# Kernel matmul steps kept a least distance apart in the planned order, with the planner's durations replaced and the third tile's arguments 128 columns wide

## The chip, the cores and the metric

The kernel runs on one core of a Trainium2 chip. The metric is the device time of one execution in microseconds. The kernel before was run three times: 387.19, 384.06 and 383.83 us, median 384.06 us. The profile is of a fourth, separate execution.

## The reference

The input is 2048 rows of width 640. Two branches work on it and a sigmoid gate of the input mixes them. The first branch is attention with 32 heads of width 20, in which row `s` looks at the eight rows `s, s-2, ..., s-14`. The second is a state-space convolution: per channel a kernel `K` of length 2048 is made from 192 complex modes, and the input is convolved with it by FFT.

```python
q, k, v = split(x @ wqkv)                        # 32 heads of 20
kg, vg = k[idx], v[idx]                          # idx = s - 2*w, w = 0..7
attn = softmax(where(mask, q . kg * 20**-0.5, -1e9))
a = (sum_w attn * vg) @ wo
P = exp(dt * A * l)                              # 640 channels x 192 modes x 2048
K = einsum("dn,dnl,dn->dl", C, P, dt * B).real
y = irfft(rfft(x, 4096) * rfft(K, 4096))[:2048] + x * Dskip
out = g * a + (1 - g) * y                        # g = sigmoid((x * gate_w).sum(-1))
```

## The kernel before

One launch holds two parts. The first part, some 300 us long, is planned: every piece of work is a `Task` with the engine it may run on, a duration, what it depends on, the buffers it takes and gives back, and a due time. `Plan.order` plays all tasks against a model of the engines, and `Plan.emit` writes the instructions in the order in which they were played and chains each engine's instructions to that order. So the instruction streams of TensorE, VectorE, ScalarE, GpSimd and the SP queue are fixed when the program is built. The durations and the numbers in `PLAN` (due times, and the small shifts `off`) decide the order and are not executed. In that model TensorE work is lengthened where too little of it (`eq`, counted in windows of 3.4133 us) was played in the window before.

The second part, some 80 us, is the FFT convolution and the final mix (`fft_conv`). It is written out by hand, is the same in both kernels and starts when the planned part has ended.

The planned part holds these streams, which share the engines:

- **Parameters** (`SSMParams.build`): elementwise work on VectorE and ScalarE over the mode parameters. It ends in twelve pieces `S`, written to memory through the SP queue.
- **Projections** (`turn`, `late`): the input is turned on TensorE, then 60 steps of five 128x512 matmuls give q, k and v (line 328). They are evicted by ScalarE or VectorE (lines 490 and 492), stored and read back by GpSimd's DMA queue.
- **Attention core**, eight blocks of 256 rows (`plan_core`): five `prod` products on VectorE (line 377) and their `lg` matmuls (383), the softmax (`max` on VectorE, `neg` on TensorE, `exp` on ScalarE at line 407, `sum` on TensorE, `at` on VectorE), a round trip through memory on the SP queue (`aS`, `asb`), five `pv` products (442), the gathering matmuls `gat` (447), the output projection `wo` (464) and its gated eviction `ga`.
- **Kernel generation**, ten chunks (`KGen.plan`). A chunk's parameters `L` are loaded by eight DMAs on the SP queue. Then, for three tiles `u` = 0, 1, 2, the argument matmuls `arg` (lines 768 and 773, into the two `ar` buffers) feed ScalarE, which takes sines (line 785) and exponentials (787). When a tile has both, VectorE makes products `pq` (808 to 810, two buffers), and four steps `kmm` per tile (826) multiply them on TensorE into the one buffer `kps`. After the third tile `fin` copies `kps` into `E` (1179) and frees it for the next chunk. Sine and exponential need different tables on ScalarE, so each change between them is a table load; the softmax needs the exponential too.
- **Expansion and first FFT stage**: after chunks 4 and 9 the sums are expanded (`own`, `move` with `nxp` at line 864, `other`), written to memory, read back as `kc`, and multiplied by a constant (`f1`, `fu`, `fk`, result `bp`, line 1195).

A tile is 128 rows of parameters wide. The parameter buffer holds 192 modes twice, so tiles 0 and 1 have 128 modes of one half each, and tile 2 is made of the remaining 64 modes of both. In the kernel before tile 2's arguments take two matmuls of 64 columns where the others take one of 128:

```python
if u < 2:      # one matmul of 128 columns
    nc.tensor.matmul(ar[:, g2, ...], L[rows, gp, sb, NST * u:NST * u + 128], R[...], tile_position=(64 * g2, 0))
else:          # two of 64
    for h in range(2):
        nc.tensor.matmul(ar[64 * h:64 * h + 64, g2, ...], L[rows, h, sb, m0:m0 + 64], R[...], tile_position=(64 * g2, 64 * h))
```

A `kmm` step of tiles 0 and 1 is 16 matmuls of 128 rows, one of tile 2 is 32 matmuls of 64 rows, each with its own weight load. The planner may play these steps as soon as the products are there, so several can stand one behind the other on TensorE.

Of the kernel before, what the change touches and what calls it, by code (L numbers as in the profile page):

```python
# [20 lines left out]
S = 2048  # L21
D = 640
H = 32
DH = 20
W = 8
# [11 lines left out]
def _attn_consts():  # L37
# [5 lines left out]
    for wp in range(W):  # L43
# [4 lines left out]
PLAN = dict(free=dict(P=4.0, A=4.2, D=4.7, S=16.0, G=16.0), phase=0.0, look=0.2, ba=85.1, bd=-687.6, grace=2235.8, p0=-791.4, p1=9.6, tx=[1364.4, 1460.7],  # L48
            txw=191.1, ql=135.4, vl=-242.7, pw=18.0, el=-653.5, tl=53.4, vw=216.1, gate=2445.0,
            l=[281.2, 189.1, 532.1, 186.3, 592.1, 47.7, -314.8, 735.8, 829.8, 993.2, 720.0, 710.4], a=[363.0, -174.6, -128.2, 185.6, 703.1, 918.9, 1303.1, 1413.4],  # L50
            v=[-164.3, -448.6, 45.4, 323.3, 710.0, 789.4, 646.8, 1095.8], g=[10.7, 292.0, -348.6, -469.5, -539.5, 427.8, 247.2, -1193.3, -158.0, -278.7, -66.5],
            dl=[129.5, 80.5, 337.8, 725.2, 614.9, 306.3, 515.6, 330.1, 400.6, 420.8],
            kl=[-352.8, -363.0, -133.2, -213.8, -584.9, -123.6, 147.3, -7.2, -17.6, -95.2], Ll=1248.1, argl=366.8, xl=1038.4, c0=1194.1, x0=1143.6, x1=118.9,
            f0=-483.5, f1=51.4, u0=914.8, u1=33.6, off={59: 46.6, 61: 84.7, 94: -58.1, 96: -12.9, 100: -8.6, 102: -29.5, 107: 10.3, 111: 11.8, 113: 8.0, 116: -14.8,
# [14 lines left out]
class Plan:  # L69
# [25 lines left out]
    def order(self):  # L95

        pr = self.pr
# [15 lines left out]
        act, table, W, done = {}, None, 3.4133, []  # L113

        def ready(t):
            x = t.rdy
            for tag in t.acq:
                k = cnt[tag] - self.SLOTS[tag]
                if k >= 0:
                    if k not in gone[tag]:  # L120
                        return None
                    x = max(x, gone[tag][k])
            return x
        for t in self.tasks:
            t.rdy = t.rdy0
        while len(done) < len(self.tasks):
# [38 lines left out]
            t.start, t.eng = x, e  # L165
            free[e] = x + d
# [38 lines left out]
class Attn:  # L205
# [22 lines left out]
    def window(self, pl, cst, pa):  # L228
# [7 lines left out]
        for n in range(2 * NKT):  # L236
            hf, kt = divmod(n, NKT)
            b = {}

            def turn(_, hf=hf, kt=kt, b=b):  # L240
                tx = b["tx"] = pa.tile([128, 2, 512], F32, name="ar")
                for i in range(8):
                    nc.tensor.matmul(tx[:, i // 4, (i % 4) * 128:(i % 4) * 128 + 128], self.xn[:, 8 * hf + i, kt * 128:(kt + 1) * 128], self.ident[:], start=True, stop=True)  # L243

            def ev(en, hf=hf, kt=kt, b=b):
                evict(nc, en, self.xT[:, hf, kt, :], b["tx"][:].rearrange("p a b -> p (a b)"))
            d = pl.pr["tx"][hf] + pl.pr["txw"] * kt
            m = pl.add(f"turn{n}", "P", 0.75, turn, acq=["ar"], due=d, eq=1024, rdy=(16.5, 26.0)[hf])
            self.xts.append((m, pl.add(f"tev{n}", "AD", {"A": 1.0, "D": 1.2}, ev, deps=[m], rel=[("ar", m)], due=d + 0.5)))
# [97 lines left out]
    def plan_core(self, pl, pvb, g_sb, ps, due0):  # L347
# [10 lines left out]
        for sc in range(S // C):  # L358
# [68 lines left out]
            sm = pl.add(f"sum{sc}", "P", 0.40, total, deps=[ex], due=due(5 * pr["pw"] + pr["el"]), eq=512)  # L427
# [4 lines left out]
            for e in range(0, 5, 2):  # L432
# [20 lines left out]
                p = lastpv = pl.add(f"pv{sc}{e}", "D", 1.11 * n, weigh, deps=[asb, vc], after=[lastpv], acq=["pv"], rel=[("vc", vc), ("asb", asb)] if e == 4 else [], due=due(pr["v"][sc] + pr["vw"] * e))  # L453
# [41 lines left out]
NST = 192  # L495
# [213 lines left out]
class KGen:  # L709
# [24 lines left out]
    def load_L(self, c):  # L734
        nc = self.nc
        L = self.Lb[c % 2]
        for g in range(4):
            for v in range(2):
                d0 = 160 * g + 80 * v + 8 * c
                src = self.prm.S[d0:d0 + 8].rearrange("(s q) i n -> (q i) s n", q=4)  # L740
                nc.sync.dma_start(L[64 * (g % 2) + 2:64 * (g % 2) + 2 + 4 * NPC, g // 2, :, NST * v:NST * v + NST], src)

    def plan(self, pl, pa, pk, start, hold, params, opened, fin):
# [5 lines left out]
        for c in range(NCH):  # L749
            d0, dd = start(c), start(c + 1) - start(c)  # L750
            L = self.Lb[c % 2]
            Lt = pl.add(f"L{c}", "S", 3.5, lambda _, c=c: self.load_L(c), deps=argt[c - 2] if c > 1 else params, due=d0 - pr["Ll"], dma=1.3)
# [3 lines left out]
            for kind in (0, 1) if c % 2 == 0 else (1, 0):  # L756
                for u in range(3):
                    ends[u, kind] = []
                    for gp in range(2):
                        for sub in range(2) if kind == 0 else (None,):  # L760
                            def args(_, u=u, kind=kind, gp=gp, sub=sub, b=b, L=L):
                                ar = b["ar"] = pa.tile([128, 2, 512], F32, name="ar")
                                for sb, a0 in ((sub, 0),) if kind == 0 else ((0, 0), (1, EW)):
                                    c0, ncol = ((0, SW), (SW, EW))[kind]
                                    for g2 in range(2):
                                        rows = slice(64 * g2, 64 * g2 + 64)
                                        if u < 2:
                                            nc.tensor.matmul(ar[:, g2, a0:a0 + ncol], L[rows, gp, sb, NST * u:NST * u + 128], R[rows, c0:c0 + ncol],  # L768
                                                             start=True, stop=True, tile_position=(64 * g2, 0))
# [20 lines left out]
                            a = pl.add(f"arg{c}{kind}{u}{gp}{sub}", "P", ((0.15, 0.15, 0.30), (0.22, 0.22, 0.40))[kind][u], args, deps=[Lt], after=[prevarg] + ([self.moved] if c == HC + 2 else []), acq=["ar"],  # L790
                                       due=due - pr["argl"], eq=(304, 432)[kind])
                            t = pl.add(f"act{c}{kind}{u}{gp}{sub}", "A", (0.62, 0.83)[kind], act, deps=[a], after=[prevact] + (hold if first and kind == 0 and ns == NTR - 1 else []), acq=[("trg", "exq")[kind]] if first else [],
# [8 lines left out]
            for u in range(3):  # L801
# [12 lines left out]
                def kmm(_, u=u, b=b, j=0):  # L814
# [4 lines left out]
                    for ql in (2 * j, 2 * j + 1):  # L819
                        for v in range(2):  # L820
                            for c2 in ((u,) if u < 2 else (0, 1)):
                                for g in range(4):
                                    r0 = 0 if u < 2 else 64 * (g // 2)
                                    rows = slice(0, 128) if u < 2 else slice(r0, r0 + 64)
                                    k = 8 * (g if u < 2 else 2 * c2 + g % 2) + ql
                                    nc.tensor.matmul(kps[32 * g:32 * g + 32, c2, NM * ql:NM * ql + NM],  # L826
                                                     pt[rows, k, v, :], qq[rows, k, v, :],
                                                     start=(g not in started), stop=(u == 2 and v == 1), skip_group_check=True,
# [5 lines left out]
                for j in range(4):  # L834
                    m = pl.add(f"kmm{c}{u}{j}", "P", 0.18 if u < 2 else 0.35, lambda e, kmm=kmm, j=j: kmm(e, j=j), deps=[p], after=[prevkmm], acq=["kb"] if u == 0 and j == 0 else [],
# [438 lines left out]
```

## Time and profile before

| | before |
|---|---|
| median of three runs | 384.06 us |
| profiled execution, device time | 384.76 us |
| its span, first to last instruction | 383.0 us |
| mean granted TensorE clock | 0.950 |
| planned part, to the first matmul of line 1024 | 0 to 301.97 us |
| `kps` matmuls (line 826) | 2560, busy 30.2 us |
| sine and exponential activations (785, 787) | 180, busy 124.9 us |

The profile gives for each engine the time in which it was busy, and for each stretch in which it was idle what ended that stretch. "Issue" means that no semaphore the profile shows held the engine. PEld is the weight loader of TensorE and runs beside its matmuls. Times are of one profiled execution. An engine's busy time in a stretch is divided by the length of the stretch to see how close to full it was. The mean duration of an activation or a vector operation is some 0.08 to 0.1 us longer than the distance from one to the next when they run back to back, because neighbours overlap.

### The profile page before, as it was taken

The numbers are of one execution on the slowest core, as the hardware profiler recorded it, in microseconds if no ns is written. First come the engines' busy times: TensorE is split into PE (matmuls) and PEld (weight loads), VectorE is DVE, ScalarE is ACT, GpSimd is POOL, SyncE is SP. The second block draws the span as 40 slices with busy tenths as digits, with TensorE's granted clock in tenths as the row PEclk, the third lists the DMA queues.
The fourth block names the chain that finished last, engine by engine and source line by source line (L and its number), as shares of the span: only waits on it lengthen the run. The fifth ranks groups of instructions, "written<-read, shape, count | busy, mean of one in ns | idle before, by whom it ended". The sixth has DMA issues, their size and how long they took to land.

```text
span 383.0 us, 11863 instructions
## 1 busy us (share of the span) xinstructions
PE 316.9 (83%) x5102; PEld 191.0 (50%) x5126; DVE 323.0 (84%) x437; ACT 304.1 (79%) x427; POOL 89.3 (23%) x122
## 2 busy tenths in 40 slices
PE   0268999998999979988997699889999899987760
PEld 0144564433445545444454344557777655656760
DVE  4879997669999989889998799999896389999782
ACT  1699884677979889789879698988987798995890
POOL 8930331140211001513653100100010022000053
PEclk9998999999999999999989757999999999998996
DMA  8982878472645233686455850403740199926056
GB/s 266 373 252 94 246 212 256 117 215 86 193 125 157 64 112 95 158 224 188 104 124 134 274 154 2 151 2 101 254 140 34 36 211 244 207 40 222 2 119 159
DMA packets 51529, 58.84 MB, mean 154 GB/s; under 512 B 36244, under 2 KB 43284, under 8 KB 51220
## 3 DMA queue, kind: packets, MB, share of 16 engines
q1 hardware_dynamic: 41492, 28.78, 28.3%
q0 software_dynamic: 8256, 28.69, 25.6%
q8 instruction: 40, 0.66, 0.7%
q10 hardware_dynamic: 1728, 0.61, 0.7%
q14 instruction: 13, 0.11, 0.1%
HBM read 38.29 MB, written 19.77 MB: 152 GB/s over the span
## 4 chain that ended last, share of the span: by engine, by line
PE 51%; ACT 19%; DVE 13%; DMA 9%; issue 5%; SPq 1%; POOL 1%; POOLq 0%; ACTq 0%; DVEq 0%
PE tb L328 13%; PE tb L447 7%; PE ar L768 6%; PE fp L1024 5%; PE tb L464 5%; PE kps L826 4%; PE bp L1195 3%; DMA aim<-in_B_A_im_dram 3%; ACT big L787 3%; ACT sp_u L1027 3%; ACT big L785 3%; PE lg L383 3%; DVE bufA L985 3%; ACT sp_k L1027 3%; PE ar L773 2%
## 5 line engine op out<-in xcount | busy, mean ns | idle before, releaser
L328 PE MATMUL tb<-bufA 128*128 128x512 bf16 x283 | 71.5, 388 | 6.5 <-DVE bufA L492 2.1
L785 ACT ACTIVATE big<-ar 128x608 bf16<-128x608 int16 x96 | 59.6, 677 | 10.2 <-PE ar L768 9.4
L787 ACT ACTIVATE big<-ar 128x864 bf16<-128x864 f32 x60 | 50.2, 897 | 4.1 <-PE ar L768 3.3
L442 DVE TENSOR_TENSOR pv<-vc,asb 128x2048 bf16<-128x2048 bf16 x40 | 47.2, 1219 | 4.3 <-PE tb L447 2.1
L328 PEld LDWEIGHTS <-bufA 128*128 128x128 bf16 x300 | 33.2, 120 | 35.1 <-issue 12.2
L377 DVE TENSOR_TENSOR prod<-qc,kc 128x2048 bf16<-128x2048 bf16 x40 | 47.9, 1219 | 2.7 <-PE lg L383 2.5
L768 PE MATMUL ar<-Rarg,L 64*128 64x304 bf16 (+1 forms) x320 | 37.0, 290 | 5.8 <-ACT big L785 2.4
L447 PE MATMUL tb<-pv,ident 128*128 128x512 bf16 (+1 forms) x185 | 39.1, 348 | 2.5 <-DVE prj L492 1.0
L826 PE MATMUL kps<-qq,pt 128*32 128x22 bf16 (+1 forms) x2560 | 30.2, 175 | 4.6 <-issue 4.2
L1024 PEld LDWEIGHTS <-PHI 128*128 128x128 bf16 x256 | 24.8, 97 | 17.6 <-issue 7.4
L826 PEld LDWEIGHTS <-pt 128*32 128x32 bf16 (+1 forms) x2560 | 23.3, 93 | 17.5 <-issue 12.3
L464 PE MATMUL tb<-wo_sb,oT 128*128 128x320 bf16 x160 | 27.7, 310 | 0.0
L768 PEld LDWEIGHTS <-L 64*128 64x128 bf16 x320 | 13.7, 94 | 27.7 <-issue 25.3
L447 PEld LDWEIGHTS <-ident 128*128 128x128 bf16 x192 | 17.8, 99 | 17.3 <-issue 5.5
L490 ACT ACTIVATE prj<-tb 128x512 bf16<-128x512 f32 x28 | 16.5, 598 | 10.9 <-PE tb L328 9.9
L959 POOL DMA_DIRECT2D PHI<-c_phi x8 | 4.5, 558 | 79.5 <-PE fp L1024 41.7
L773 PE MATMUL ar<-Rarg,L 64*64 64x304 bf16 (+1 forms) x320 | 19.6, 298 | 3.8 <-ACT big L787 1.6
L1027 ACT ACTIVATE sp_k<-fp 128x1280 bf16<-128x1280 f32 x16 | 19.1, 1236 | 3.3 <-PE fp L1024 3.0
L810 DVE TENSOR_TENSOR qq<-big 128x1408 bf16<-128x1408 bf16 x24 | 21.3, 886 | 0.0
L1024 PE MATMUL fp<-bufA,PHI 128*128 128x320 bf16 x128 | 19.1, 298 | 2.3 <-ACT sp_u L1027 1.5
L243 PE MATMUL ar<-ident,xn 128*128 128x128 bf16 x80 | 7.9, 263 | 15.6 <-DMA xn<-in_A_x_dram 14.1
L1024 PE MATMUL fp<-big,PHI 128*128 128x320 bf16 x128 | 19.2, 298 | 1.8 <-ACT sp_k L1027 1.8
(201 smaller groups left out, 633.0 us busy)
## 6 DMA issues: line engine op xcount, KB each, us to landing
asb<-aS SPq DMA_DIRECT2D x8, 512.0 KB, 4.0
PSI<-c_psi SPq DMA_DIRECT2D x8, 512.0 KB, 10.2
PHI<-c_phi POOLq DMA_DIRECT2D x8, 384.0 KB, 6.6
Sprm<-pc SPq DMA_DIRECT2D x12, 240.0 KB, 3.7
L<-Sprm SPq DMA_DIRECT2D x80, 36.0 KB, 2.6
kc<-kS POOLq DMA_DIRECT2D x8, 337.5 KB, 4.7
vc<-vS POOLq DMA_DIRECT2D x8, 337.5 KB, 4.9
xn<-in_A_x_dram SPq DMA_DIRECT2D x4, 640.0 KB, 12.4
```

The source lines that it names most:

```text
L328: nc.tensor.matmul(ppf, self.wq[:, kt, which * D + e:(which + 1) * D:5], self.xT[:, c0 // 1024, kt, c0 % 1024:c0 % 1024 + SC], start=(kt = ...
L377: nc.vector.tensor_tensor(b[e][:], b["qc"][:, e, :].unsqueeze(1).to_broadcast([128, W, C]), win(b["kc"][:, e, :], 0, W, DIL, C), ALU.mult)
L442: nc.vector.tensor_tensor(b["pv", e][:, :, k, :].rearrange("p w (b t) -> p w b t", t=64), for_e, aw, ALU.mult)
L447: nc.tensor.matmul(b["op", e][:, 0:n, :], ident[:], b["pv", e][:, w, 0:n, :], start=(w == 0), stop=(w == W - 1))
L464: nc.tensor.matmul(apf[:, :320], b["oT"][:, e, i * 128:(i + 1) * 128], wo_sb[:, e, hf * 320:(hf + 1) * 320], start=(e == 0), stop=(e == 4))
L768: nc.tensor.matmul(ar[:, g2, a0:a0 + ncol], L[rows, gp, sb, NST * u:NST * u + 128], R[rows, c0:c0 + ncol], start=True, stop=True, tile_pos ...
L773: nc.tensor.matmul(ar[64 * h:64 * h + 64, g2, a0:a0 + ncol], L[rows, h, sb, m0:m0 + 64], R[rows, c0:c0 + ncol], start=True, stop=True, til ...
L785: nc.scalar.activation(dst[:, 2 * gp:2 * gp + 2, sub, :], ar[:].bitcast(I16)[:, :, 0:2 * SW:2], ACT.Sin, scale=SCL)
L787: nc.scalar.activation(dst[:, 2 * gp:2 * gp + 2].rearrange("p g s n -> p g (s n)"), ar[:, :, 0:2 * EW], ACT.Exp)
L826: nc.tensor.matmul(kps[32 * g:32 * g + 32, c2, NM * ql:NM * ql + NM], pt[rows, k, v, :], qq[rows, k, v, :], start=(g not in started), stop ...
L1024: nc.tensor.matmul(fp[:, fl, 0:320].rearrange("p (c x) -> p c x", x=32), PHI[:, fl, kind, :], B[:, :, 2 * f1 + ri].rearrange("p c q g -> p ...
L1027: nc.scalar.activation(t[:], fp[:, :, 0:320].rearrange("p f (x g) -> p x f g", g=4), ACT.Identity)
```

## The change

The order of the planned part is made anew, and three things differ in what is executed or how it is ordered.

- **Distance.** When a `kmm` step is played at time `x`, the next one may not be played before `x + kg`, or `x + 2 * kg` after a step of the tile that has 32 matmuls (`kg` is 0.6). This exists in the planner alone; no wait is added to the program.
- **Tile order and width.** The parameters are laid out in the buffer so that the two 64-mode remainders stand side by side and form tile 1. All tiles then take one matmul of 128 columns for an argument. 320 matmuls of 64 columns become 160 of 128, and 160 weight loads go with them. The 32-matmul `kmm` steps move from tile 2 to tile 1, their number is unchanged. `load_L` still issues eight DMAs of the same size.
- **Durations and plan numbers.** Durations of the tasks `turn`, `max`, `sum`, `pv`, `L`, `arg`, `act` and `kmm` are set to other values, and nearly all numbers of `PLAN` are others.

```diff
-PLAN = dict(free=dict(P=4.0, A=4.2, D=4.7, S=16.0, G=16.0), phase=0.0, look=0.2, ba=85.1, bd=-687.6, grace=2235.8, p0=-791.4, p1=9.6, tx=[1364.4, 1460.7],
+PLAN = dict(free=dict(P=4.0, A=4.2, D=4.7, S=16.0, G=16.0), phase=0.0, kg=0.6, look=0.2, ba=37.5, bd=-770.3, grace=2320.2, p0=-773.3, p1=8.0, tx=[1409.2, 1314.0],
...
-        act, table, W, done = {}, None, 3.4133, []
+        act, table, W, done, nextk = {}, None, 3.4133, [], 0.0
 
         def ready(t):
-            x = t.rdy
+            x = max(t.rdy, nextk) if t.name.startswith("kmm") else t.rdy
...
             t.start, t.eng = x, e
+            if t.name.startswith("kmm"):
+                nextk = x + pr["kg"] * (2 if t.dur["P"] > 0.2 else 1)
...
-            m = pl.add(f"turn{n}", "P", 0.75, turn, acq=["ar"], due=d, eq=1024, rdy=(16.5, 26.0)[hf])
+            m = pl.add(f"turn{n}", "P", 0.5, turn, acq=["ar"], due=d, eq=1024, rdy=(16.5, 26.0)[hf])
...
-            mx = pl.add(f"max{sc}", "D", 0.90, top, deps=[l], due=due(5 * pr["pw"]))
+            mx = pl.add(f"max{sc}", "D", 1.09, top, deps=[l], due=due(5 * pr["pw"]))
...
-        for g in range(4):
+        for g in range(2):
             for v in range(2):
-                d0 = 160 * g + 80 * v + 8 * c
-                src = self.prm.S[d0:d0 + 8].rearrange("(s q) i n -> (q i) s n", q=4)
-                nc.sync.dma_start(L[64 * (g % 2) + 2:64 * (g % 2) + 2 + 4 * NPC, g // 2, :, NST * v:NST * v + NST], src)
+                for h in range(2):
+                    d0 = 160 * ((2 * v + g + 2 * h) % 4) + 80 * h + 8 * c
+                    src = self.prm.S[d0:d0 + 8].rearrange("(s q) i n -> (q i) s n", q=4)
+                    l0 = NST * (h ^ v)
+                    nc.sync.dma_start(L[64 * g + 2:64 * g + 2 + 4 * NPC, :, v, l0:l0 + NST], src)
...
-                                        if u < 2:
-                                            nc.tensor.matmul(ar[:, g2, a0:a0 + ncol], L[rows, gp, sb, NST * u:NST * u + 128], R[rows, c0:c0 + ncol],
-                                                             start=True, stop=True, tile_position=(64 * g2, 0))
-                                        else:
-                                            m0 = NST * gp + 128
-                                            for h in range(2):
-                                                nc.tensor.matmul(ar[64 * h:64 * h + 64, g2, a0:a0 + ncol], L[rows, h, sb, m0:m0 + 64], R[rows, c0:c0 + ncol],
-                                                                 start=True, stop=True, tile_position=(64 * g2, 64 * h))
+                                        l0 = 128 * (2 - u if gp else u)
+                                        nc.tensor.matmul(ar[:, g2, a0:a0 + ncol], L[rows, sb, gp, l0:l0 + 128], R[rows, c0:c0 + ncol],
+                                                         start=True, stop=True, tile_position=(64 * g2, 0))
...
-                            for c2 in ((u,) if u < 2 else (0, 1)):
+                            for h in (0, 1) if u == 1 else (u // 2,):
...
-                    m = pl.add(f"kmm{c}{u}{j}", "P", 0.18 if u < 2 else 0.35, lambda e, kmm=kmm, j=j: kmm(e, j=j), deps=[p], after=[prevkmm], acq=["kb"] if u == 0 and j == 0 else [],
+                    m = pl.add(f"kmm{c}{u}{j}", "P", 0.25 if u == 1 else 0.13, lambda e, kmm=kmm, j=j: kmm(e, j=j), deps=[p], after=[prevkmm], acq=["kb"] if u == 0 and j == 0 else [],
```

In the instruction streams this gives, by engine:

| stream | before | after |
|---|---|---|
| TensorE: argument matmuls | 640 | 480 |
| TensorE: runs of `kps` matmuls with nothing between them | 65 | 118 |
| of these, runs of 48 matmuls and more | 21 | 1 |
| ScalarE: table loads | 17 | 21 |
| ScalarE: evictions `oT` 512 / `oT` 256 / `prj` 512 / `ga` / `nxt` | 15 / 4 / 28 / 16 / 2 | 12 / 5 / 27 / 19 / 4 |
| VectorE: evictions `oT` 512 / `oT` 256 / `prj` 512 / `ga` / `nxt` | 1 / 4 / 17 / 16 / 2 | 4 / 3 / 18 / 13 / 0 |
| TensorE after the last `nxp`, in the planned part: `bp` / `wo` / `gat` matmuls | 112 / 55 / 48 | 100 / 50 / 48 |

More of the change, by code (lines that the diff above doesn't have):

```diff
@@ L820, in kmm @@
                         for v in range(2):
-                            for c2 in ((u,) if u < 2 else (0, 1)):
+                            for h in (0, 1) if u == 1 else (u // 2,):
                                 for g in range(4):
[L823 to L826, printed above, removed]
+                                    r0 = 64 * (g // 2) if u == 1 else 0
+                                    rows = slice(r0, r0 + 64) if u == 1 else slice(0, 128)
+                                    k = 8 * ((g + 2 * h) % 4) + ql
+                                    nc.tensor.matmul(kps[32 * g:32 * g + 32, h, NM * ql:NM * ql + NM],
                                                      pt[rows, k, v, :], qq[rows, k, v, :],
-                                                     start=(g not in started), stop=(u == 2 and v == 1), skip_group_check=True,
+                                                     start=(g not in started), stop=(v == 1 and u == 1 + h), skip_group_check=True,
                                                      tile_position=(r0, 32 * g))
```

25 lines of the change are left out of this document (14 added, 11 removed), and 3 rows, old and new, of the table f0.

## The prediction

> **What bounds the kernel now.** First, busy time by engine and the granted clock (the page's parts 1 and 2), and the packets of the instruction queue (part 3).
>
> ```profile
> PE 316.9 (83%) x5102; PEld 191.0 (50%) x5126; DVE 323.0 (84%) x437; ACT 304.1 (79%) x427; POOL 89.3 (23%) x122
> ...
> PEclk9998999999999999999989757999999999998996
> ...
> q8 instruction: 40, 0.66, 0.7%
> ```
>
> Three engines are about equally full, and the clock dips in the middle. Second, busy time by stage, from the table of windows (stretch, its length, then busy time and count for PE, PEld, DVE, ACT, POOL, then clock, DMA share, GB/s).
>
> ```profile
> 74.00:92.00 18.00, 16.66 (x127) 7.36 (x126) 13.60 (x18) 14.23 (x23) 4.17 (x5) 1.00 0.50 149
> 92.00:140.00 48.00, 44.93 (x1097) 23.36 (x1106) 46.43 (x63) 42.49 (x62) 6.83 (x8) 1.00 0.44 126
> 140.00:198.00 58.00, 52.39 (x1154) 28.15 (x1155) 53.19 (x77) 50.16 (x80) 20.95 (x21) 1.00 0.53 143
> 198.00:218.50 20.50, 15.06 (x392) 8.36 (x382) 15.58 (x27) 15.24 (x22) 6.33 (x12) 0.83 0.74 202
> 218.50:235.50 17.00, 15.67 (x336) 6.72 (x334) 16.68 (x22) 16.03 (x24) 0.00 (x0) 0.50 0.39 113
> 235.50:269.00 33.50, 30.92 (x749) 19.99 (x749) 32.50 (x45) 28.88 (x40) 2.86 (x4) 1.00 0.27 80
> 269.00:301.90 32.90, 31.29 (x224) 23.93 (x224) 26.04 (x37) 26.83 (x35) 1.80 (x3) 1.00 0.36 117
> ```
>
> From 92 to 269 us VectorE sets the pace: its idle time there is 1.6 + 4.8 + 4.9 + 0.3 + 1.0 = 12.6 us, against 18.0 on TensorE and 24.2 on ScalarE. From 269 on TensorE is 95% busy and VectorE waits. So an edit pays where it removes VectorE idle before 269, or TensorE work after. VectorE's largest idle is in 198 to 218.5. Third, the timeline there.
>
> ```profile
> 212.62 0.64 PE L826 MATMUL kps<-qq,pt 64*32 64x22 bf16 x63
> 215.88 0.41 PE L826 MATMUL kps<-qq,pt 64*32 64x22 bf16 x33 [2.61 <-issue]
> 216.70 1.37 ACT L785 ACTIVATE big<-ar 128x608 bf16<-128x608 int16 x2 [2.60 <-PE ar L768]
> 217.26 0.53 DVE L1179 CAST E<-kps 128x352 bf16<-128x352 f32 x1 [2.41 <-PE kps L826]
> ```
>
> TensorE stands 2.61 us inside a run of `kps` matmuls that waits for no semaphore, and both other engines wait for it. I read this as waiting for instructions. The queue named instruction moved 40 packets of 16 KB while TensorE ran 5102 + 5126 instructions: 256 per packet. In TensorE's order the stops inside `kps` runs (0.79 us at 136.7, 0.34 at 155.1, 0.46 at 196.5, 2.61 at 213.3) are each a whole number of 256 instructions apart, and before the largest, 256 instructions were used up in about 2.8 us, with DMA full. Fourth, the clock around two of them, in windows of 3.41 us.
>
> ```profile
> 194.56:197.97 3.41, 2.66 (x161) 1.89 (x158) 3.38 (x11) 3.38 (x6) 3.41 (x3) 0.99 0.02 5
> 197.97:201.38 3.41, 3.41 (x38) 1.56 (x27) 3.10 (x7) 1.53 (x2) 1.05 (x2) 0.51 1.00 230
> 211.62:215.04 3.42, 1.65 (x74) 1.03 (x70) 3.23 (x4) 2.47 (x3) 0.00 (x0) 0.99 1.03 327
> 215.04:218.45 3.41, 2.57 (x79) 1.15 (x79) 0.88 (x2) 1.43 (x3) 1.68 (x3) 0.50 0.64 211
> ```
>
> After each the clock is halved; after the second it stays so to 235.5. But from 218.5 to 235.5 VectorE is busy 98%: the slow clock there hides behind it.
>
> **The distance between steps.** The new order breaks up the runs: of 65 runs of `kps` matmuls 21 had 48 or more, now 118 runs and one such. A run of 16 beside one argument step is 36 instructions, and ScalarE takes a sine step in 0.59 us (four take 2.45, the last of them 0.68), so 256 instructions last some 4 us instead of 2.8. What the stops cost the path is VectorE's wait behind each. The stop of 2.61: 2.41. The one of 0.79: at most its length, 0.8, of VectorE's 1.29 at 141.98 (waiting for a late projection). The one of 0.34: 0.34 of 1.37 at 156.33 (waiting for `kps`). The one of 0.46 halves the clock, and ten `wo` matmuls then take 2.82 us instead of 1.47 (their row at 248.11): 1.35 of VectorE's 1.55 at 203.51. A further 0.52 at 128: 0.16. The half clock after 218.5: 0.3. Sum 5.4; bounds 0 and 5.4.
>
> [...]
>
> Against it stands that short runs are dearer. A run of 16 takes 0.20 us, of 32 0.30, of 64 0.58 from start to next start: beginning a run costs 0.05 to 0.10. 53 more runs are 2.7 to 5.3 us on TensorE, which has 18 us idle in the stretch. Bounds 0 and 5.3; I take 1.0, nearer to nothing because VectorE is the fuller engine.
>
> **The wider arguments.** By their rows a step of four 64-column matmuls at 304 wide takes 0.255 us from start to next start and two of 128 take 0.235; at 216 wide 0.31 and 0.29. 40 x 0.02 + 20 x 0.02 = 1.2 us less TensorE work. Bounds 0 and 1.2; I take 0.6. The eight loads of `L` have the same size and stay behind the same SP queue; their landing ends few waits (0.6 us on the weight loader).
>
> **The order made anew.** VectorE's work changes by evictions alone: `oT` +3 x 0.60 - 0.34, `prj` +0.60, `ga` -3 x 0.46, `nxt` -0.80 = -0.1 us; nothing. ScalarE gets `ga` +3 x 0.46, `nxt` +0.71, `oT` +0.31 - 3 x 0.50, `prj` -0.50 = +0.4, and four table loads. They lie at the second and third softmax (87 to 101 us before), which now cut into a sine phase. A load takes 1.28 us and costs 1.41 with the lost overlap (the activation before it starts at 73.50, the next at 75.41, normal distance 0.50): 5.6 us. In 74 to 140 ScalarE is busy 86%, and its 9.3 us of waits there are mostly for TensorE; behind the loads stand argument activations, so TensorE's `ar` buffers too. Bounds 0 and 5.6; I take 2.5. [...]
>
> After the last `nxp`, where TensorE sets the end, 12 `bp` matmuls (0.11 each) and five `wo` (0.68 together) fewer remain: 2.0 us. They are done earlier, beside a full VectorE. Bounds 0 and 2.0; I take 2.0. The read-back of the last `kc` is still covered: about as much TensorE work as before (19 us) stands between `nxp` and its first use, and the transfers took some 15; beyond 19 every us would be on the end.
>
> GpSimd's queue has `kc` behind the store of `vS` for block 0; vS was stored at 48.8, two loads of 0.87 and 4.7 to land give 55.3, against the first `prod` at 55.2. Nothing: VectorE has parameter work beside it until 56.7; were that done first, each us that `kc` lands later would be one of VectorE's.
>
> **Sum.** -5.4 + 1.0 - 0.6 + 2.5 - 2.0 = -4.5. The profiled execution took 384.76 us (span 383.0 and 1.8 around it), so 380.3; the median of the runs is 0.7 lower, 384.06, so **379.6 us**.
>
> **Rivals.**
> - *The loads and the short runs eat the gain.* All 5.6 and half of 5.3 on the path: -5.4 + 2.7 - 0.6 + 5.6 - 2.0 = +0.3: 384.4. For it: every engine is close to full in 92 to 140. Against: ScalarE's 9.3 us of waits. [...]
> - *Slower: the spread steps hold their buffers.* Products have two buffers, `kps` has one. Bunched, four steps of a tile end within 0.58 to 1.2 us; spread by 0.6 or 1.2 each they end 2 to 4 us later, and VectorE, in order, waits at the next products or at `fin`, with `prod` and `pv` queued behind. If each of ten chunks adds 1.0 us, -4.5 + 10 = 389.6. It decides the sign from 0.45 us per chunk on. For: `E` waited for `kps` 3.8 us already. Against: the order never has three products in a row on VectorE any more, where the old one has.
> - *Much faster: even feeding removes half of VectorE's remaining idle.* 12.6 - 5.4 leaves 7.2, and 4.4 in 74 to 92; half is 5.8: 373.8.
> - *It doesn't do what it says: the stops stay.* If they come from full DMA queues rather than from dense instructions, spreading doesn't help: +0.9, 385.0. For: DMA share 1.03 at the largest. Against: at 196.5 it was 0.02. [...]
>
> **How the numbers follow.** A measurement can tell about 1% (3.8 us) from no change; the edge is 380.2. Forecast 0.40, with 0.27 below the edge and 0.13 above; loads 0.17 (0.13 same, 0.04 slower); spread steps 0.22 (0.18 slower, 0.04 same); even feeding 0.13, faster; stops stay 0.08 (0.06 same, 0.01 on each side). Faster 0.41, same 0.36, slower 0.23. The range goes from 373, which takes in most of the even feeding, to 389.5, where the spread steps have half their cases: about 2 in 10 lie outside.
>
> **What would show it.** Right: TensorE's issue waits inside `kps` below 1 us in sum, the clock at 1.00 from 198 to 235, VectorE idle in 92 to 269 near 8 us, the planned part ending near 297. Wrong: VectorE waiting for `kps` at `E` or at products in most chunks; ScalarE above 95% in 74 to 140; a half clock in other places; a new wait for `kc`.

## The result, and the profile after

The kernel after takes 381.06 us (median of 20 runs, 378.47 to 384.41) where the kernel before takes 384.80 beside it (20 runs, 382.70 to 388.06). The ratio is 0.9901, with a 95% interval of 0.9876 to 0.9926: some 3.7 us less, where the prediction had 4.5. The profiled execution took 382.15 us, span 380.4, against 384.76 and 383.0.

First come the same three lines of the page: busy time by engine, granted clock, instruction packets.

```profile
PE 319.4 (84%) x4938; PEld 190.8 (50%) x4966; DVE 323.0 (85%) x435; ACT 307.8 (81%) x433; POOL 92.6 (24%) x122
...
PEclk9998999999999999986969989999999999998995
...
q8 instruction: 39, 0.64, 0.7%
```

TensorE has 160 matmuls fewer in the program (164 in the records of the trace, in which some are missing) and is busy longer, VectorE does the same work, and the clock still dips, at other places. Second, the table of windows, with the same columns as before.

```profile
74.00:92.00 18.00, 16.21 (x111) 7.26 (x110) 13.38 (x17) 15.52 (x23) 3.32 (x4) 1.00 0.44 142
92.00:140.00 48.00, 46.37 (x827) 23.21 (x834) 44.02 (x62) 44.04 (x65) 6.74 (x9) 1.00 0.44 132
140.00:198.00 58.00, 51.26 (x1264) 26.62 (x1265) 52.95 (x78) 52.09 (x78) 27.56 (x27) 0.86 0.57 133
198.00:218.50 20.50, 18.86 (x422) 10.29 (x423) 19.92 (x27) 18.56 (x30) 3.29 (x5) 0.99 0.75 236
218.50:235.50 17.00, 15.02 (x276) 7.18 (x277) 15.38 (x21) 14.73 (x23) 1.41 (x2) 0.90 0.29 82
235.50:269.00 33.50, 31.86 (x782) 20.78 (x784) 32.12 (x49) 29.26 (x41) 1.40 (x2) 1.00 0.30 94
269.00:299.00 30.00, 28.52 (x204) 21.73 (x203) 23.27 (x28) 23.94 (x33) 1.79 (x3) 1.00 0.34 111
```

From 198 to 218.5, where the stop of 2.61 us was, VectorE is now idle for 0.6 us where it was idle for 4.9. But in 92 to 140 it is idle for 4.0 where it was 1.6, and in 218.5 to 235.5 for 1.6 where it was 0.3. Over 92 to 269 its idle time is 12.6 us, as before. What it waits for has changed. These are VectorE's longest waits from 92 to 269 us, first of the kernel before (in total, times, longest), then of the kernel after.

```profile
DVE E L1179 <- PE kps L826: 3.8, 2, 2.4
DVE pt L808 <- ACT big L787: 1.8, 2, 1.5
DVE pt L808 <- ACT big L785: 1.7, 3, 0.8
DVE prj L492 <- PE tb L328: 1.5, 2, 1.3
```

```profile
DVE prj L494 <- PE tb L330: 3.5, 3, 1.6
DVE oT L494 <- PE tb L449: 3.4, 4, 1.2
DVE pv L444 <- PE tb L449: 1.5, 1, 1.5
```

Of the waits of kernel generation, that at `E` is gone, and of those of the products `pt` 1.5 us are left where there were 3.8. Evictions that wait for projection and gathering matmuls stand in their place: in 92 to 140 TensorE is busy for 46.37 of 48 us, and two `prj` copies there wait 1.65 and 1.10 us. The longest waits at `pv` and `oT` come right behind, 1.50 at 142.52 and 1.23 at 144.97.

The time came from two other places. The first is VectorE's start. Its work up to 92 us, by the windows of the kernel before, then of the kernel after (third busy column):

```profile
0.00:92.00 92.00, 67.37 (x476) 36.25 (x485) 71.58 (x87) 64.16 (x88) 35.83 (x51) 0.98 0.71 218
```

```profile
0.00:92.00 92.00, 68.25 (x471) 36.80 (x480) 74.49 (x90) 64.93 (x87) 35.65 (x51) 0.98 0.72 219
```

By 92 us VectorE has done 2.9 us more work than it had before (its busy time in 40 to 74 us is 31.73 where it was 27.64). Up to the last copy of `E` it has 1.3 us more to do in all (237.2 us where it was 236.0), so that copy starts 1.8 us earlier, at 267.22 (before: 269.00). TensorE, which is full there, takes longer from the copy to the last `nxp` (2.04 us, before 0.88), so that `nxp` starts only 0.6 us earlier, at 269.26 (269.88). The second place is the tail: from there to the first `fp`, the first matmul of the FFT part, it is 29.8 us where it was 32.1. So the planned part ends at 299.08 instead of 301.97, 2.9 us earlier, of which the tail has 2.3. The FFT part takes 81.3 us, before 81.0.

### The profile page after: what moved, and what is told of

Read it like the earlier page. It is cut to its first block, busy times and chain, and to the rows that moved or that the text cites. A ratio compares the mean times of both kernels' runs of the same rounds, so it can differ in the third digit from the quotient of the medians.

```text
span 380.4 us, 11537 instructions
## 1 busy us (share of the span) xinstructions
PE 319.4 (84%) x4938; PEld 190.8 (50%) x4966; DVE 323.0 (85%) x435; ACT 307.8 (81%) x433; POOL 92.6 (24%) x122
## 4 chain that ended last, share of the span: by engine, by line
PE 29%; ACT 16%; DVE 7%; issue 3%; POOL 1%; DMA 1%; POOLq 0%; ACTq 0%; DVEq 0%
PE tb L449 6%; PE fp L1023 5%; PE bp L1194 5%; ACT big L784 5%; PE tb L466 4%; PE ar L772 3%; ACT sp_u L1026 3%; DVE bufA L984 3%; ACT sp_k L1026 3%; PE kps L825 2%; PE yp L1076 2%; ACT big L786 1%; ACT bufA L784 1%; POOL out_dram L1090 1%; DVE prod L379 1%
## 5 line engine op out<-in xcount | busy, mean ns | idle before, releaser
L772 PE MATMUL ar<-Rarg,L 64*128 64x304 bf16 (+1 forms) x480 | 56.0, 289 | 10.5 <-ACT big L784 4.2
L784 ACT ACTIVATE big<-ar 128x608 bf16<-128x608 int16 x96 | 58.3, 682 | 3.2 <-PE ar L772 2.6
L786 ACT ACTIVATE big<-ar 128x864 bf16<-128x864 f32 x60 | 49.4, 895 | 1.2 <-PE ar L772 1.0
L772 PEld LDWEIGHTS <-L 64*128 64x128 bf16 x480 | 22.0, 95 | 41.7 <-issue 37.2
L825 PE MATMUL kps<-qq,pt 128*32 128x22 bf16 (+1 forms) x2560 | 37.0, 174 | 1.7 <-issue 1.5
L825 PEld LDWEIGHTS <-pt 128*32 128x32 bf16 (+1 forms) x2560 | 25.1, 93 | 25.5 <-issue 17.1
L1026 ACT ACTIVATE sp_u<-fp 128x1280 bf16<-128x1280 f32 x16 | 19.1, 1237 | 1.8 <-PE fp L1023 1.8
L370 POOL DMA_DIRECT2D vc<-vS x8 | 7.0, 880 | 48.2 <-DVE pv L444 39.5
```

The source lines that it names most:

```text
L772: nc.tensor.matmul(ar[:, g2, a0:a0 + ncol], L[rows, sb, gp, l0:l0 + 128], R[rows, c0:c0 + ncol], start=True, stop=True, tile_position=(64 ...
L784: nc.scalar.activation(dst[:, 2 * gp:2 * gp + 2, sub, :], ar[:].bitcast(I16)[:, :, 0:2 * SW:2], ACT.Sin, scale=SCL)
L786: nc.scalar.activation(dst[:, 2 * gp:2 * gp + 2].rearrange("p g s n -> p g (s n)"), ar[:, :, 0:2 * EW], ACT.Exp)
L825: nc.tensor.matmul(kps[32 * g:32 * g + 32, h, NM * ql:NM * ql + NM], pt[rows, k, v, :], qq[rows, k, v, :], start=(g not in started), stop= ...
L1026: nc.scalar.activation(t[:], fp[:, :, 0:320].rearrange("p f (x g) -> p x f g", g=4), ACT.Identity)
```

## The experiments

Twelve more kernels were run beside the kernel before, each six times, and a_bunch, a_narrow and b_start twelve times. In the table "stops" is TensorE's issue time at `kps` matmuls in the profile (in brackets the number of stops), "planned end" the start of the first `fp`. Names with a_ are edits of the kernel after, with b_ of the kernel before. Line numbers differ a little from kernel to kernel.

| kernel | median, before's median beside it (us) | ratio, 95% interval | stops (us) | planned end |
|---|---|---|---|---|
| before | 384.80 | 1 | 4.2 (4) | 301.97 |
| after | 381.06, 384.80 | 0.9901, 0.9876 to 0.9926 | 1.5 (2) | 299.08 |
| a_kg0 | 411.82, 387.12 | 1.0645, 1.0585 to 1.0704 | 11.1 (9) | 327.2 |
| a_bunch | 386.77, 386.00 | 1.0012, 0.9980 to 1.0044 | 2.7 (4) | 302.6 |
| a_noload | 382.15, 387.12 | 0.9880, 0.9827 to 0.9932 | 0.7 (1) | 299.0 |
| a_narrow | 385.71, 386.00 | 0.9998, 0.9965 to 1.0030 | 1.2 (1) | 305.5 |
| b_kg | 394.02, 387.12 | 1.0222, 1.0157 to 1.0286 | 1.8 (1) | 311.0 |
| b_wide | 391.58, 387.12 | 1.0126, 1.0078 to 1.0174 | 3.7 (4) | 310.4 |
| b_spread | 393.17, 386.00 | 1.0198, 1.0162 to 1.0234 | 5.3 (5) | 310.8 |
| b_start | 388.24, 386.00 | 1.0048, 1.0013 to 1.0083 | 5.9 (5) | 306.9 |
| b_sh64 | 396.08, 386.36 | 1.0266, 1.0208 to 1.0323 | 8.6 (6) | 315.2 |
| b_sh128 | 398.39, 386.36 | 1.0292, 1.0224 to 1.0360 | 8.1 (7) | 311.1 |
| a_sh64 | 379.57, 386.36 | 0.9868, 0.9813 to 0.9923 | 0.7 (1) | 296.9 |
| a_sh128 | 382.22, 386.36 | 0.9888, 0.9825 to 0.9950 | 1.6 (2) | 301.1 |

### The distance taken out, and put in alone

**a_kg0** is the kernel after, planned with the distance at zero.

```diff
-phase=0.0, kg=0.6, look=0.2
+phase=0.0, kg=0.0, look=0.2
```

> The changed kernel with kg set to 0 in the plan and nothing else: runs of kps matmuls fall from 118 to 58, 26 of them with 48 or more, and ScalarE has 23 table loads instead of 21. Theory (the distance is worth what the stops cost less the dearer short runs, 5.4 - 1.0 = 4.4 us): 381.0 + 4.4, some 385.5 us, ratio to before 1.00, stops of over 0.3 us inside kps runs are back and sum to 2 us or more. Rival (the gain comes from the other plan numbers, the distance is worth nothing): 381 us, ratio 0.99, whether stops are back or not.

It is 6.45% slower than before, far outside both expectations, some 26 us above the theory. The largest stop in the trace is in a run of `kps` matmuls:

```profile
146.30 0.39 PE L825 MATMUL kps<-qq,pt 128*32 128x22 bf16 x29 [3.74 <-issue]
```

Nine such stops add up to 11.1 us; two more before argument matmuls to 3.0. So the new plan needs its distance, and without it the stops come back. But the order as a whole is another, and VectorE waits 9.55 us at one `ga` and 6.90 us at one `pv` for TensorE, so this run does not price the stops.

**b_kg** is the kernel before with the distance of 0.6 in the planner, and nothing else (the number in `PLAN` and the planner lines of the change).

> The kernel before with the distance alone (kg 0.6, old plan numbers, durations and tiles): 116 runs of kps matmuls, one of 48 or more, 20 table loads instead of 17. Theory: the stops vanish, -5.4 + 1.0, and three loads cost 1.9: -2.5 us, ratio 0.993. Rival (the plan numbers carry the gain, and the old ones do not suit the distance): ratio 1.00 to 1.02 though the stops are gone.

One stop of 1.8 us is left, and the kernel is 2.2% slower, just above the rival's range. VectorE's longest single wait in the planned part is now `pv` for the load of `vc`, 3.0 us; in sum its evictions of `bp` wait 7.2 us for TensorE, and `E` waits 2.8 us for `kps`. A likely reason, not shown, is that the due times of the old plan do not suit the new order. Fewer stops alone do not make this kernel faster.

### Each other part alone

**b_wide** is the kernel before, its own order, with the new layout and the wide arguments.

```diff
-for h in range(2):
-    nc.tensor.matmul(ar[64 * h:64 * h + 64, g2, ...], L[rows, h, sb, m0:m0 + 64], ...)
+l0 = 128 * (2 - u if gp else u)
+nc.tensor.matmul(ar[:, g2, ...], L[rows, sb, gp, l0:l0 + 128], ...)
```

> The kernel before with the 128-column layout alone: the order on VectorE and ScalarE is unchanged, TensorE has 320 instructions fewer in the same order of steps. Theory (a little less TensorE work, 0 to 1.2 us, which is not the bound): ratio 0.997 to 1.000. Rival (fewer instructions are what counts, since TensorE stands waiting for them): ratio 0.990 to 0.995 and the stops inside kps runs fall to about half.

A miss for both: with 320 instructions fewer on TensorE it is 1.3% slower. The stops are elsewhere; one of 3.8 us stands before an `lg` matmul, where all `lg` matmuls together had 0.4 in the kernel before.

**a_noload** is the kernel after with the `exp` of the second and third softmax replaced by a scaled copy on the same engine and at the same place, so that no table is loaded for them (17 loads in place of 21). It leaves out the exponential of these two blocks, so its attention there is not the reference's.

```diff
-nc.scalar.activation(b["at"][:], b["lg"][:], ACT.Exp, scale=scale)
+nc.scalar.activation(b["at"][:], b["lg"][:], ACT.Identity if sc in (1, 2) else ACT.Exp, scale=scale)
```

> The changed kernel in its own order, but the softmax exponentials of blocks 1 and 2 are replaced by a scaled copy, so that the four table loads around them are gone; the attention of these two blocks is left out in effect. Theory (2.5 of the 5.6 us lie on the path): 378.5 us, ratio to before 0.983. Rival 1 (the loads hide wholly): 381 us, 0.990. Rival 2 (they lie wholly on the path): 375.4 us, 0.976.

ScalarE's busy time in the two stretches of the loads (fourth busy column) falls by 5.3 us, from 15.52 and 44.04:

```profile
74.00:92.00 18.00, 16.60 (x118) 6.98 (x117) 11.87 (x16) 12.78 (x20) 3.32 (x5) 1.00 0.45 142
92.00:140.00 48.00, 47.61 (x817) 23.15 (x816) 44.59 (x61) 41.52 (x63) 6.64 (x8) 1.00 0.44 133
```

The planned part ends at 299.02 in place of 299.08, and the ratio cannot be told from that of the kernel after. The four loads cost nothing that can be measured. That they lie wholly on the path (0.976) is ruled out; the two intervals together still leave room for some 3 us, so the 2.5 of the theory is unlikely and not excluded.

**a_narrow** is the kernel after, with its order, but the old layout, loads and two 64-column matmuls (the second diff above in reverse); the 32-matmul steps go back to the third tile with it.

> The changed kernel with the third tile's arguments, its loads and its kernel matmuls as they were before the change (two 64-column matmuls in place of one of 128, 320 matmuls more); the order of all steps is the changed kernel's. Theory (the wide arguments are worth nearly nothing by themselves): 0.988 to 0.994 of the kernel before, the planned part's end within 1.2 us of 299.1. Rival (fewer instructions on TensorE are what feeds it in time): issue waits inside kps of 4 us or more, and 0.998 to 1.02.

The gain is gone: 0.9998. The time is the rival's, but not by stops, which take 1.2 us. TensorE is busy 6.0 us longer (325.4 against 319.4), and it is at half clock longer:

```profile
140.00:198.00 58.00, 52.32 (x1221) 25.99 (x1222) 52.66 (x78) 51.23 (x76) 18.85 (x26) 0.79 0.60 134
198.00:218.50 20.50, 18.73 (x373) 10.25 (x376) 17.09 (x25) 17.26 (x26) 3.90 (x6) 0.83 0.50 147
```

The clock is 0.79 and 0.83 where it was 0.86 and 0.99. Up to the planned end, the half clock lasts 37.6 us in this profile and 23.9 in that of the kernel after. Of the 6.4 us by which the planned part ends later, 5.1 are there when the sixth copy of `E` starts (208.19 against 203.05), after products waited 1.8 us for `kps` and 1.1 for an activation. This profiled execution took 388.09 us, 2.4 above the median of its kernel, so its 6.4 us is more than the usual loss. On this order the wide arguments are worth about 1% of the time, the layout and the order of the step sizes included, which the run does not separate. That the longer half clock is what costs the time is likely and not shown by itself.

### Bunched and spread, with the other engines' order kept

**a_bunch** is the kernel after with the four steps of a tile moved together.

```diff
+for t in [t for t in od if t.name.startswith("kmm") and t.name[-1] == "3"]:
+    mates = [m for m in od if m.name[:-1] == t.name[:-1] and m is not t]
+    for m in mates:
+        od.remove(m)
+    i = od.index(t)
+    od[i:i] = mates
```

> The changed kernel with each tile's four kernel-matmul steps brought together where its last one stands; the order on VectorE, ScalarE, GpSimd and SyncE is the changed kernel's own, and so are loads and widths. TensorE's kernel matmuls then stand in 30 runs (20 of 64, 10 of 128). Theory (the long runs make TensorE stop for instructions, and the distance is what took that away): issue waits inside kps go from 1.5 us to 8 us or more, with single ones above 2 us, and the time stands at 1.015 to 1.06 of the kernel before. Rival (the gain lies in the order on VectorE and ScalarE, the distance does little): issue waits inside kps stay under 4 us and the time at 0.985 to 1.0 of the kernel before.

The ratio lies between the two expectations: 1.0012, so bunching costs 1.1%. The stops are 2.7 us in sum: within the rival's bound of 4, far from the theory's 8. Two of them, in TensorE's timeline:

```profile
152.72 0.54 PE L836 MATMUL kps<-qq,pt 64*32 64x22 bf16 x51 [1.23 <-issue]
...
158.09 0.26 PE L836 MATMUL kps<-qq,pt 128*32 128x22 bf16 x13 [0.90 <-issue]
```

VectorE waits 3.5 us at `E` for `kps` and 5.1 at products (2.6 for `kps`, 2.5 for what the profile calls issue). Only part of this can be stops: a tile's steps now all stand at the place of its last one, which makes `fin` and the next products late by themselves. What of the 1.1% is which remains open.

**b_spread** is the reverse on the kernel before: the four steps of a tile are put apart as far as the fixed order of VectorE, ScalarE and the queues allows.

> The kernel before with its kernel-matmul steps spread out as far as its own order on the other engines allows (96 runs where it had 65, 8 of 64 and no longer one, where 21 or so were); nothing else is touched, so VectorE's, ScalarE's and both queues' orders are the same. Theory (the stops are worth what they cost): issue waits inside kps fall from 4.2 us to 2 us or less, VectorE's idle time between 198 and 218 us falls by 2 us or more, the planned part ends 1.5 to 4 us earlier, the time is 0.985 to 0.996 of the kernel before. Rival (what is won at the stops is given back where a later step is late): the issue waits fall as well, but the time is 0.997 to 1.02.

A miss for both on the stops, which grow to 5.3 us in `kps`, 3.1 in arguments and 1.7 in gathering matmuls; the time is that of the rival. So the number of runs (96 in place of 65) is not what decides. What the trace shows of the reason is under "Where the blocks of instructions end": at six of the seven stops of 0.35 us and more the packet of instructions itself started late, by the measure given there (2.1 us and more).

**b_start** is the kernel before with three projection steps behind the fifth score step, meant to fill VectorE's idle time at 40 to 74 us.

```diff
+late = [t for t in od if t.name in ("late26", "late27", "late28", "lev26", "lev27", "lev28", "lst12")]
...
+i = next(i for i, t in enumerate(od) if t.name == "lg04") + 1
+od[i:i] = late
```

> The kernel before with three of the projection steps (and their copies and one store) moved behind the fifth score step, so that VectorE has copies to do while it waits for scores between 40 and 74 us, as in the changed kernel; nothing else moves. Theory (part of the gain is VectorE's idle time in 40 to 74 us, 6.4 us before and 2.3 after): idle time there falls to 4.5 us or less and the time is 0.990 to 0.996 of the kernel before. Rival (time won there is waited for later, since later steps hang on ScalarE or TensorE): 0.998 to 1.004.

It does not do what it was made for: VectorE is busy 27.61 us in 40 to 74, as before (27.64), and the time is slightly longer, just above the rival's range. Whether VectorE's better start alone brings the gain of the kernel after is not shown.

### Where the blocks of instructions end

If the stops come at every 256th instruction, it should matter where in the order these edges fall, and a kernel can be given other edges without touching its work. Tiny matmuls were put into TensorE's idle time between 3 and 15 us, writing a corner of a tile that nothing reads: 32 of them move all that follows by 64 instructions (**b_sh64**, **a_sh64**), 64 by 128 (**b_sh128**, **a_sh128**).

```diff
 nc.scalar.activation(gw_sb[:], lt[:, 0, 5:10], ACT.Identity)
+for _ in range(64):
+    nc.tensor.matmul(lt[:, 1, 0:10], lg10[:], ident[0:10, 0:10], start=True, stop=True)
```

> The kernel before with 64 tiny matmuls (128 instructions with their weight loads) put into TensorE's idle time between 3 and 15 us; they write a corner of a tile that nothing reads. Nothing else changes, so every later TensorE instruction stands 128 places later in its own order. Theory (the stops fall where TensorE's instruction order crosses a multiple of 256 inside a run of kernel matmuls): the stops move to other matmuls, by half a block, and the time leaves that of the kernel before by 0.5% or more, slower likelier than faster since its order was made with the stops where they were: 1.005 to 1.02. Rival (where the edges fall has no bearing): stops at the same matmuls, 0.997 to 1.003.

> The changed kernel with the same 64 tiny matmuls in the same idle time. Theory (short runs need no luck with the edges): issue waits inside kps stay under 3 us, none above 1.2 us, and the time is 0.986 to 0.995 of the kernel before. Rival (the changed kernel is as much made for its edges as the one before, and won by them): 0.996 to 1.01.

> As the first, with 32 tiny matmuls, 64 places. Theory: stops at other matmuls again, 1.003 to 1.02. Rival: 0.997 to 1.003.

> The changed kernel with 32 tiny matmuls, 64 places. Theory: 0.986 to 0.995, issue waits inside kps under 3 us. Rival: 0.996 to 1.01.

The kernel before becomes 2.7 and 2.9% slower, more than the theory gave; the kernel after stays where it was (one stop of a_sh128, 1.36 us, is longer than the 1.2 that was expected at most). A shift by a whole block of 256, after which by this count the edges would fall as before, was not run. The first copy of `E` is at 120.64 and 120.50 us in the shifted kernels before, 120.20 in the unshifted, so the added matmuls cost nothing at their own place. The loss comes later. TensorE's timeline of b_sh128:

```profile
202.15 0.45 PE L828 MATMUL kps<-qq,pt 64*32 64x22 bf16 x37
203.84 0.37 PE L828 MATMUL kps<-qq,pt 64*32 64x22 bf16 x27 [1.25 <-issue]
...
217.94 0.72 PE L464 MATMUL tb<-wo_sb,oT 128*128 128x320 bf16 x4
220.75 0.31 PE L464 MATMUL tb<-wo_sb,oT 128*128 128x320 bf16 x1 [2.09 <-issue]
220.99 0.93 PE L828 MATMUL kps<-qq,pt 64*32 64x22 bf16 x96
221.85 0.43 PE L770 MATMUL ar<-Rarg,L 64*128 64x304 bf16 x2
222.22 0.38 PE L828 MATMUL kps<-qq,pt 64*32 64x22 bf16 x29
224.48 0.20 PE L828 MATMUL kps<-qq,pt 64*32 64x22 bf16 x3 [1.88 <-issue]
```

Runs of 37 and 27, and of 29 and 3, are steps cut in two. The stop at 220.75 is among `wo` matmuls: it is no property of the `kps` matmul but of the place in the order. Counted in the program's order, with a weight load and a matmul as two instructions, the stops at 203.84, 220.75 and 224.48 stand at instructions 5564, 6076 and 6332, all with remainder 188 after division by 256. The matmul after the largest stop of the kernel before, at 215.88, has the number 6076 too, though it is another matmul. Some matmul records are missing from the traces, but the weight loads are all there (5126 before, 4966 after), one for each matmul. Counted by them, 59 of the 61 stops of 0.35 us and more from 40 us to the planned end, in all fourteen kernels, stand at exactly this remainder, the four of the kernel after and its two shifted forms among them. The other two are 0.35 us each. Such a place is called an edge here.

The traces also hold the packets of the instruction queue, and they show what comes ahead of a stop at an edge. At each of the 59 stops TensorE goes on 1.16 to 1.61 us after a packet has landed that had started behind the edge before. At these stops, then, the next 256 instructions started on their way only after TensorE had begun on the 256 before them, and two things are seen there:

- *The block is used up fast.* In 26 stops the packet starts promptly, within 1.6 us of the edge before. The medians are 1.1 us to its start, 1.1 for its transfer and 1.4 until TensorE goes on, an estimated 3.6 us in all (their sum). From 92 us to the planned end the kernel before uses up ten of 30 blocks in less than 3.5 us (shortest 2.57), the kernel after none (3.75), its shifted forms none (3.52 in both). b_sh64 has a block of 2.23, b_sh128 one of 1.64.
- *The packet is late.* In 29 stops it starts 2.1 to 5.3 us after the edge before, while the DMA engines are between half busy and full (at the two stops of the kernel after it starts 2.12 and 3.76 us after, with a DMA share of 0.89 and 0.93 in that time). All four stops of the kernel after and its shifted forms are of this kind, and six of the seven of b_spread. Four more stops lie between the two kinds. The stop of 2.61 us in the kernel before is of both: its block was used up in 2.67 us, and its packet started after 3.20, with a DMA share of 1.03. That full DMA engines make a packet late is not shown: in the kernel before, the packets ahead of the stops at 137.50 and 247.57 started after 1.23 and 0.98 us at a share of 0.92 and 0.91.

So what counts in these runs is how fast a whole block goes by and when the next packet starts, and not how long one run is. VectorE pays behind such stops: in b_sh64 `E` waits 6.8 us for `kps`, 3.8 in the kernel before, none after. In b_sh128 that wait is 3.2 us, and longer ones are at a late projection (3.37) and at scores (2.92). The half clock lasts 48 us up to the planned end of b_sh64 and 34 in b_sh128, 27 in the kernel before.

## Why the prediction was right, and where it was not

**The stops (-5.4).** That TensorE stops for instructions at edges 256 apart is shown: the shifted runs move the stops to other matmuls at the same remainder. With the steps kept apart, no block is used up in less than 3.75 us (2.57 before), and the stops fall from 4.2 to 1.5 us inside `kps` and from 0.9 to none elsewhere. The reading "dense instructions" was half of it; the largest stop had a late packet as well, and the 1.5 us that are left have late packets alone ahead of them (they started 2.12 and 3.76 us after the edge, and their blocks took 3.93 and 5.16 us to use up). The stages named by the prediction got their time: VectorE's idle time in 198 to 218.5 fell by 4.3, its wait at `E` from 3.8 to none. Wrong was that it would stay won. The prediction asked for VectorE's idle time in 92 to 269 near 8 us; it is 12.6, as before. Inside `kps` it asked for less than 1 us of issue waits and for a planned end near 297; 1.5 and 299.1 came. The new plan has other late things: `prj` and `oT` evictions and a `pv` product that wait for TensorE, which is 97% busy in 92 to 140. The term was costed wait by wait on the old order, and a new order has its own.

**Dearer short runs (+1.0).** `kps` matmuls take 37.0 us in place of 30.2, so TensorE paid 6.8 where the upper bound was 5.3 (part of it at half clock: 14.40 us of the 37.0 lie in 140 to 198, at a clock of 0.86). What came on the path cannot be read alone; the 2.4 us by which VectorE's idle time grew in 92 to 140 are not from there, as `kps` is busy less in that stretch (7.47 against 8.81 us, 528 matmuls recorded in place of 768).

**The wider arguments (-0.6, bounds 0 and 1.2).** Mis-sized: a_narrow puts them at some 3.7 us of 386 (0.9998 less 0.9901), layout and step order included. The price of a step was read at full clock; with the narrow matmuls TensorE was at half clock longer in the one trace, and behind them stand activations and products. On the old order the same part is 1.3% slower, so it has no price apart from the order.

**The table loads (+2.5).** Probably mis-sized: a_noload shows no gain from taking them out, though its interval leaves room for some of the 2.5. ScalarE had 9.3 us of waits in the stretch, and these likely took the loads in. The first rival needed all 5.6 us of them on the path, and falls with that.

**The tail (-2.0).** Right: 32.1 to 29.8 us, -2.3.

**The sum.** Ahead of the last `nxp` the terms gave -2.5 and the trace shows -0.6; behind it -2.0 and -2.3. The forecast of 379.6 us came within 1.5 of 381.06. That the terms before `nxp` came so near to the measured size is partly luck: -5.4 was mostly given back, +2.5 was hardly paid, -0.6 was too small, and VectorE's 2.9 us of work done earlier, by 92 us, was no term at all.

**The rivals.** Spread steps that hold their buffers: no wait at `E` is left, so this did not happen. Stops that stay because queues are full: most went, so as a forecast of the time it failed, but all stops that stayed have a late packet, those of the kernel after at a DMA share of 0.89 and 0.93; that full queues make it late is not shown. Even feeding, 373.8: not reached, VectorE's idle time from 92 to 269 us is what it was.

**The clock.** The prediction asked for 1.00 from 198 to 235. It is 0.99 and 0.90; the half clock moved to 168 to 178, 192 to 198 and 222 to 226 and shrank from 27 to 24 us up to the planned end, so part of the wrong sign (a half clock in other places) came. The working let the stop of 0.46 halve the clock; the stop of 0.79 has no half clock behind it, and the rows at the end show a half clock without a stop.

**What the prediction did not see.** The kernel before owes part of its time to where its edges fall. Moved by 64 or 128 instructions it takes 2.7 or 2.9% more. Every other single edit of it that was run was slower as well (1.0048 to 1.0222); how much of that is edges is not shown. The stops were costed as a fixed toll of 5.4 us, while the order of before has its edges where the toll is smaller than at the two other positions that were tried. The change made the time nearly free of these edges (0.9901, 0.9868 and 0.9888 at three positions, with overlapping intervals), and that is its larger worth; the gain of 1% is against the old kernel at the best of three positions. a_sh64 is the lowest, but its interval does not set it apart from the kernel after.

## What to carry to other kernels

Count the instructions of an engine, not only its busy time: where small matmuls used up 256 instructions faster than the next were brought (an estimated 3.6 us here, longer where the packet started late), TensorE stopped in these runs, for up to 3.9 us. A few idle instructions ahead of the work show in one run how much of a kernel's time hangs on where these edges fall (2.7 and 2.9% for the kernel before). A fixed order holds such positions without showing them, so a part of a change tried on the old order alone may measure moved edges as well; try it on both. Waits won at one place count only when the next late thing behind them is known.

## What the runs showed of the hardware

- The stops are up to 3.9 us long inside `kps` runs (b_start), 3.83 before an `lg` matmul (b_wide) and 2.09 among `wo` matmuls (b_sh128). The packets of the instruction queue fit blocks of 256: 40 packets for 10252 weight loads and matmuls before (256.3 each), 39 for 9932 after (254.7).
- Up to the planned end the granted clock is halved for stretches of 3.41, 3.41 and 20.48 us in the trace of the kernel before, and of 3.41, 10.24, 6.83 and 3.41 in that of the kernel after: one, one and six, and one, three, two and one times 3.41. Three times it was halved right after a window of this length in which TensorE was busy for 1.91 to 2.36 us. These three windows of the kernel after that stand right ahead of a half clock in 40 to 299 us, then one of the kernel before that does not:

```profile
164.23:167.64 3.41, 1.91 (x64) 1.21 (x61) 3.41 (x5) 3.40 (x6) 3.41 (x1) 1.00 0.06 16
188.12:191.54 3.42, 2.36 (x76) 1.18 (x76) 3.42 (x6) 3.42 (x7) 3.15 (x6) 1.00 1.00 256
218.84:222.25 3.41, 1.98 (x42) 1.21 (x42) 3.41 (x6) 2.72 (x6) 0.00 (x0) 1.00 0.81 226
```

```profile
201.31:204.72 3.41, 2.34 (x31) 1.24 (x30) 1.86 (x3) 2.91 (x4) 2.03 (x5) 1.00 0.44 110
```

TensorE's busy time is the first busy column; VectorE is full in each of the three, and DMA is at 0.06 in one and at 1.00 in another. In the third it also stops for instructions, 0.88 us. The busy time of a window does not decide by itself: after the fourth, with 2.34 us, the clock stays whole, and the prediction's window at 194.56, with 2.66, has a half clock behind it. What decides is not shown.
